# A new written-out order for the first twelve steps, with six weight signs on VectorE, two buffers of C, one of v, and weights laid out by pieces

## The chip, the cores and the metric

The kernel runs on one NeuronCore of one Trainium2 chip. The metric is the device time of one execution in microseconds (us). The kernel before takes 920.79 us, the median of three runs (920.3 to 921.5). The engines are named as in the profile: PE is TensorE, DVE is VectorE, ACT is ScalarE, POOL is GpSimd, SP is the engine that issues the DMAs here.

## The reference, cut to what matters

```python
# attention within chunks of 64 rows: q, k, v are 8 batches x 8 heads x 576 x 64, fp32
scores = q_c @ k_c^T / sqrt(64);  attn = softmax(scores) (sum + 1e-9);  out = attn @ v_c
# heads side by side: x is 4608 x 512; w_in is 512 x 2048, w_out 2048 x 512, both float64
h = x @ w_in
P = a[0] + a[1]*h + a[2]*h**2 + a[3]*h**3
Q = 1 + |b[0]|*|h| + |b[1]|*h**2
y = (P / (Q + 1e-6)) @ w_out          # fp32 out, 4608 x 512
```

## The kernel before, in words

The 4608 rows are cut into 18 blocks of 256 rows, and the 2048 hidden columns into 4 quarters. A block with a quarter is a *step*; there are 72. Each block first needs its attention, each step a first product (ff1), an elementwise chain and a second product (ff2).

Precision comes from splitting: x, the weights and g are each held as a high and a low part in the reduced fp32 type, and a product is three matmuls (high by high, high by low, low by high). One ff1 is 48 matmuls of 128x256 (line 334); one ff2 is counted as 48 rows by the profile (line 405).

The weights arrive as float64 and are turned into the two parts on the chip. They come in 16 pieces of 1 MB: pieces 0-3, 6, 7, 10, 11 are of w_in, the others of w_out, two pieces for each quarter. A piece goes through a buffer called `raw`, of which there are three, shared with the q and k loads of later blocks. On a piece run, in this order: `s` scales the upper words as fp32 (ACT, line 159), `o` shifts the lower words (DVE, line 155), `i` writes the sign of the scaled value over the top of the lower word by a cast to fp16 (ACT, line 163), `j` joins the words to an fp32 value (DVE, line 167), `h` writes the high part (ACT, line 170), and `d` the low part (DVE, line 175). For three pieces the low part is made by PE and ACT instead (`r`, lines 183 and 184, and `l`, line 190). `d` or `r` sets the buffer free, and the next `w` (line 144) that waits for it in SP's queue may then start.

The order of the whole work is fixed. For the first twelve steps (blocks 0 and 1 interleaved, then block 2) and the attention of blocks 0 to 3 it is written out by hand in `START`: every item is a letter and a number, and each engine works through its own items in the order of the list. The other letters: `q`, `v`, `k` load q with k, v, and the constants; `S M U E n N T K A X Y` are the attention of a block (scores, maximum, subtraction, exponential, sums, normalisation, transpose, copy, product with v, high and low part of x); `F f` are the two halves of a step's ff1; `a b c I J` are its ACT part, `Q p P g H R G` its DVE part; `Z z y` are the three parts of its ff2 (the last with the low part of g); `O` stores a block. After the list a loop runs steps 12 to 71 in a fixed pattern, with ff2 two steps behind ff1.

What ties the engines together around the change: the results of ff1 lie in PSUM, bank pair `p0` for steps 0 to 9 save step 1, so that the next ff1 there waits until `P` of the step before has read it; `G`, the last item of a chain on DVE, must come before `y`; tile C of the chain has one buffer, so `c` (line 346) waits until the `R` of the chain before has read it.

Of the kernel before, what the change touches and what calls it, by code (L numbers as in the profile page):

```python
# [9 lines left out]
F32 = mybir.dt.float32  # L10
# [3 lines left out]
ALU = mybir.AluOpType  # L14
# [3 lines left out]
P = 128  # L18
UPB = 2
NB = 18  # L20
BT = 128 * UPB
# [4 lines left out]
FPS = 4  # L26
NST = DFF // (128 * FPS)
W = FPS * BT
# [2 lines left out]
EXP_WIDE = (0, 1)  # L31

START = (
# [12 lines left out]
)  # L46
FIRST = 12
CUT_FIRST, CUT_LAST = 24, 48
# [6 lines left out]
def tile_chunked_attention_rational_moe(  # L55
# [11 lines left out]
    nc = tc.nc  # L67
    cp = ctx.enter_context(tc.tile_pool(name="cp", bufs=1))
    p2 = ctx.enter_context(tc.tile_pool(name="p2", bufs=2))
# [14 lines left out]
    a0, a1, a2, a3 = (ab[:, i:i + 1] for i in range(4))  # L84
    b0, b1a = ab[:, 4:5], ab[:, 6:7]
# [24 lines left out]
    def load_v(n):  # L110
        if n >= NB:
            return
        v = p2.tile([P, W], F32, tag="vt", name=f"v{n}")
        nc.sync.dma_start(out=v, in_=vP[n])
        loaded["v", n] = v

# [18 lines left out]
    def w_load(j):  # L135
        raws[j] = raw = p2.tile([P, W, 2], I32, tag="raw", name=f"raw{j}", bufs=3)
        out, fq, k = PIECES[j]
        if out:
            c = 4 * fq + 2 * k
            src = w_out[c * P:(c + 2) * P, :]  # L140
        else:
            src = w_in[:, 1024 * fq + 512 * k:1024 * fq + 512 * k + 512]
        src = src.rearrange("(c p) (f w) -> p c f w", p=P, w=2)
        nc.sync.dma_start(out=raw.rearrange("p (c f) w -> p c f w", c=src.shape[1]), in_=src)

    def words(j):
        low, high = raws[j][:, :, 0], raws[j][:, :, 1]
        return low, high, high.bitcast(F32)
# [12 lines left out]
    def w_sign(j):  # L161
        upper = raws[j].bitcast(mybir.dt.float16).rearrange("p f (w h) -> p f w h", h=2)[:, :, 0, 1]
        nc.scalar.copy(upper, words(j)[2])  # L163

    def w_join(j):
        low, high, val = words(j)
        nc.vector.scalar_tensor_tensor(high, high, 3, low, ALU.logical_shift_left, ALU.bitwise_or)
# [152 lines left out]
    ch, gbuf, obuf = {}, {}, {}  # L320
# [21 lines left out]
        nc.scalar.activation(ch[n, s][2], ch[n, s][0], AF.Square)  # L342

    def chain_c(n, s):
        ch[n, s][3] = p2.tile([P, FPS, BT], F32, tag="C", name=f"C{n}_{s}", bufs=1)
        nc.scalar.activation(ch[n, s][3], ch[n, s][0], AF.Identity, bias=a2, scale=a3)  # L346

    def chain_q(n, s):
# [96 lines left out]
    def qk(n, u=None):  # L445
# [5 lines left out]
    of_step = lambda f: lambda g: f(*steps[g])  # L451
    do = {
        "k": consts, "B": abs_b1, "q": qk, "v": load_v, "w": w_load,
        "o": w_low, "s": w_scale, "j": w_join, "i": w_sign, "h": w_hi, "d": w_lo_dve, "r": w_rest, "l": w_lo,
        "S": att_s, "M": att_max, "U": att_sub, "E": att_exp, "n": att_rs, "N": att_norm,
        "T": att_t, "K": att_copy, "A": att_av, "X": att_xhi, "Y": att_xlo,
        "O": store,
# [5 lines left out]
    for letter, f in zip("abcQIJpPgHRG", (  # L463
        chain_a, chain_b, chain_c, chain_q, chain_ln, chain_exp,
        chain_p, chain_p2, chain_ghi, chain_r1, chain_r2, chain_glo,
    )):
        do[letter] = of_step(f)
# [9 lines left out]
    for g in range(FIRST, total + LAG):  # L477
        n, s = steps[min(g, total - 1)]
        m, stage = n + 1, s if n + 1 < NB and g < total else None
        one = lambda letters, k: run(" ".join(f"{x}{k}" for x in letters))  # L480
        if g < total:
            one("Ffab", g)
            if stage == 1:
                one("nN", m)
            one("cQ", g)
            if stage == 0:
                one("SMU", m)
                load_qk(m + 1)
            if stage == 2:
                one("A", m)  # L490
                load_v(m + 1)
            one("IJpP", g)
            if stage == 0:
                one("E", m)
            if stage == 2:
                one("X", m)
            one("gHRG", g)
            if stage == 2:
                one("Y", m)
        back = steps[g - LAG]  # L500
        one("Zzy", g - LAG)
        if back[1] == NST - 1:
            store(back[0], last=(back[0] == NB - 1))
        if stage == 1:
            one("TK", m)
# [32 lines left out]
```

## Time and profile before

| | |
|---|---|
| median of the runs | 920.79 us |
| the profiled execution | 920.15 us, of which the span from first to last instruction is 918.3 us |
| PE, DVE, ACT busy in the span | 874.2, 747.0, 593.4 us |
| mean granted TensorE clock | 0.983 of full speed |
| DMA | 55.87 MB in the span |

The span holds one execution; some 1.85 us of the profiled time lie outside of it. Busy times are sums of single instructions with their overlaps taken once. In the rows of groups a number of us is the group's busy time and the number in ns the mean of one instruction. The chain of waits is followed back from the last instruction, and names for each moment what the end was waiting for.

### The profile page before, as it was taken

To read this page: it belongs to the slowest core of one execution; us is meant where nothing else is said; L and a number is where in the kernel's file an instruction comes from. 1 tells how busy PE (TensorE), PEld (TensorE's weight loads), DVE (VectorE), ACT (ScalarE), POOL (GpSimd) and SP (SyncE) were. 2 spreads that over 40 slices of the span, in tenths; PEclk is the share of its full clock that TensorE was granted. 3 is DMA by queue.
4 is the path that set the end of the run, shared out by engine and by line. 5 is a ranking of instruction groups with operands and counts; after the bars stand their busy time and mean duration, and the time that the engine had idled before them with its cause. 6 is when DMAs were issued, how large, how long until landed. Compare 5 with 4: busy or idle time off the path is not lost.

```text
span 918.3 us, 21052 instructions
## 1 busy us (share of the span) xinstructions
PE 874.2 (95%) x9378; PEld 859.6 (94%) x9378; DVE 747.0 (81%) x668; ACT 593.4 (65%) x984; POOL 0.8 (0%) x8
## 2 busy tenths in 40 slices
PE   4579799999999999999999999999999999999997
PEld 2578789999999999999999999999999999999997
DVE  5688888799888878787878787878788887888884
ACT  5999697757575757575757565656565656566452
POOL 0000000000000000000000000000000000000000
PEclk9679999999999999999999999999999999999999
DMA  8443522112010111102020203020202020101011
GB/s 294 164 161 138 170 92 84 27 45 58 36 59 36 41 54 26 69 14 80 4 91 1 93 1 93 2 93 1 93 2 93 2 93 2 47 1 25 1 24 24
DMA packets 20601, 55.87 MB, mean 61 GB/s; under 512 B 2592, under 2 KB 2592, under 8 KB 20512
## 3 DMA queue, kind: packets, MB, share of 16 engines
q1 hardware_dynamic: 20512, 54.54, 18.3%
q8 instruction: 73, 1.20, 0.5%
q14 instruction: 16, 0.13, 0.0%
HBM read 45.09 MB, written 9.44 MB: 59 GB/s over the span
## 4 chain that ended last, share of the span: by engine, by line
PE 82%; ACT 11%; DVE 2%; DMA 2%; issue 1%; SPq 1%; ACTq 0%
PE po L405 39%; PE ph L334 38%; ACT raw L163 3%; PE psx L207 2%; PE pss L207 2%; DMA raw<-in_w_in 2%; ACT raw L159 2%; PE pst L286 1%; ACT e L262 1%; ACT A L339 1%; ACT wo_hi L170 1%; ACT A L354 1%; ACT B L342 1%; ACT C L346 1%; ACT A L358 1%
## 5 line engine op out<-in xcount | busy, mean ns | idle before, releaser
L334 PE MATMUL ph<-xhi,wi_hi 128*128 128x256 f32 x1152 | 325.2, 282 | 10.1 <-DVE C L366 6.7
L334 PE MATMUL ph<-xlo,wi_hi 128*128 128x256 f32 x1152 | 322.3, 280 | 1.6 <-DVE xlo L317 1.6
L334 PE MATMUL ph<-xhi,wi_lo 128*128 128x256 f32 x1152 | 321.5, 279 | 0.0
L339 ACT ACTIVATE A<-ph,ab 128x1024 f32<-128x1024 f32 x72 | 81.1, 1126 | 264.6 <-PE ph L334 263.2
L405 PE MATMUL po<-wo_hi,ghi 128*128 128x256 f32 (+2 forms) x1152 | 228.9, 280 | 3.2 <-DVE ghi L371 3.2
L334 PEld LDWEIGHTS ph<-xhi,wi_hi 128*128 128x128 f32 x1152 | 219.4, 190 | 11.6 <-issue 5.8
L405 PE MATMUL po<-wo_lo,ghi 128*128 128x256 f32 x1152 | 225.6, 277 | 0.0
L334 PEld LDWEIGHTS ph<-xlo,wi_hi 128*128 128x128 f32 x1152 | 219.7, 191 | 2.2 <-DVE xlo L317 2.2
L334 PEld LDWEIGHTS ph<-xhi,wi_lo 128*128 128x128 f32 x1152 | 219.6, 191 | 0.0
L405 PEld LDWEIGHTS po<-wo_hi,ghi 128*128 128x128 f32 x1152 | 174.1, 188 | 5.7 <-DVE ghi L371 3.4
L350 DVE SCALAR_TENSOR_TENSOR B<-B,ab,A 128x1024 f32<-128x1024 f32 x72 | 92.4, 1284 | 103.0 <-ACT B L342 103.0
L405 PEld LDWEIGHTS po<-wo_lo,ghi 128*128 128x128 f32 x1152 | 174.4, 189 | 0.0
L405 PE MATMUL po<-wo_hi,glo 128*128 128x256 f32 (+2 forms) x1152 | 143.3, 277 | 1.6 <-DVE glo L383 1.6
L405 PEld LDWEIGHTS po<-wo_hi,glo 128*128 128x128 f32 x1152 | 136.5, 188 | 2.1 <-DVE glo L383 1.8
L371 DVE SCALAR_TENSOR_TENSOR ghi<-C,ab,A 128x1024 fp32r<-128x1024 f32 x72 | 92.4, 1284 | 11.0 <-ACT A L358 2.4
L354 ACT ACTIVATE A<-B,cst 128x1024 f32<-128x1024 f32 x72 | 83.8, 1165 | 26.3 <-DVE B L350 26.3
L366 DVE SCALAR_TENSOR_TENSOR C<-C,ab,ph 128x1024 f32<-128x1024 f32 x72 | 92.2, 1280 | 3.2 <-ACT B L342 1.0
L379 DVE SCALAR_TENSOR_TENSOR B<-C,ab,B 128x1024 f32<-128x1024 f32 x72 | 92.5, 1284 | 2.4
L383 DVE TENSOR_TENSOR glo<-B,A 128x1024 fp32r<-128x1024 f32 x72 | 88.2, 1225 | 6.8
L362 DVE TENSOR_TENSOR C<-C,ph 128x1024 f32<-128x1024 f32 x72 | 87.5, 1215 | 4.5 <-ACT B L342 3.6
L375 DVE SCALAR_TENSOR_TENSOR B<-B,ghi 128x1024 f32<-128x1024 f32 x72 | 88.2, 1224 | 2.3
L346 ACT ACTIVATE C<-ph,ab 128x1024 f32<-128x1024 f32 x72 | 87.8, 1220 | 2.2 <-DVE B L379 2.0
(53 smaller groups left out, 708.8 us busy)
## 6 DMA issues: line engine op xcount, KB each, us to landing
v<-in_vP SPq DMA_DIRECT2D x18, 512.0 KB, 4.0
out<-o SPq DMA_DIRECT2D x72, 128.0 KB, 2.4
raw<-in_w_in SPq DMA_DIRECT2D x8, 1024.0 KB, 6.6
raw<-in_w_out SPq DMA_DIRECT2D x8, 1024.0 KB, 5.5
qk<-in_qT SPq DMA_DIRECT2D x16, 512.0 KB, 4.6
qk<-in_kT SPq DMA_DIRECT2D x16, 512.0 KB, 5.5
Aqk<-in_qT SPq DMA_DIRECT2D x2, 256.0 KB, 3.6
Bqk<-in_kT SPq DMA_DIRECT2D x2, 256.0 KB, 4.4
```

The costliest lines, as they stand in the source:

```text
L334: nc.tensor.matmul(ph[:, fi, :], w[:, cc, f], x[:, cc, :], start=(k == 0), stop=(k == len(mm) - 1))
L339: nc.scalar.activation(ch[n, s][1], ch[n, s][0], AF.Abs, scale=b0)
L346: nc.scalar.activation(ch[n, s][3], ch[n, s][0], AF.Identity, bias=a2, scale=a3)
L350: nc.vector.scalar_tensor_tensor(B, B, b1a, A, ALU.mult, ALU.add)
L354: nc.scalar.activation(A, B, AF.Ln, bias=cst[:, 0:1], scale=2.0 ** -KLN)
L362: nc.vector.tensor_mul(C, C, h)
L366: nc.vector.scalar_tensor_tensor(C, C, a1, h, ALU.add, ALU.mult)
L371: nc.vector.scalar_tensor_tensor(gbuf[n, s][0], C, a0, A, ALU.add, ALU.mult)
L375: nc.vector.scalar_tensor_tensor(B, B, CQ, gbuf[n, s][0].bitcast(F32), ALU.add, ALU.mult)
L379: nc.vector.scalar_tensor_tensor(B, C, a0, B, ALU.add, ALU.subtract)
L383: nc.vector.tensor_mul(gbuf[n, s][1], B, A)
L405: nc.tensor.matmul(obuf[n][:, i, cols], g[:, fi, i * 128:(i + 1) * 128], w[:, FPS * s + fi, cols], start=start, stop=stop,)
```

## The change: what it does

- The list `START` has the same 383 items save for these: the sign of pieces 2, 3, 4, 5, 10 and 13 is made by a new item `e` on DVE (the sign bit of the upper word is or-ed into the lower word) instead of `i` on ACT; the low part by PE and ACT is made for pieces 6, 7 and 10 instead of 1, 7 and 9, so that `d` moves from 6 and 10 to 1 and 9. All items stand in a new order. It begins with the load of piece 3, and the loads of block 1's q and k and of the constants come later. Pieces are loaded in the order 3, 0, 1, 4, 2, 12, 5, 6, 7, 8, 9, 10, 13, 11, 14, 15; before it was 1, 3, 0, 4, 5, 8, 2, 7, 6, 9, 12, 13, 10, 14, 11, 15.
- Tile C gets two buffers, v one instead of two.
- The host lays out each weight piece as 128 rows of 8 KB. Before, a piece of w_in was read in runs of 2 KB, and one of w_out in runs of 4 KB.

```diff
-    "q0.1 q0.0 w1 q1 S0.0 S0.1 M0.0 U0.0 w3 k0 s1 o1 M0.1 E0.0 U0.1 i1 n0.0 w0 S1 E0.1 j1 n0.1 h1 N0.0 v0 s3 r1 "
-    "o3 M1 v1 i3 N0.1 s0 U1 w4 l1 o0 T0.0 j3 i0 T0.1 K0.0 j0 h3 K0.1 d3 h0 A0.0 w5 E1 d0 A0.1 X0.0 o4 s4 Y0.0 w8 "
-    "n1 X0.1 i4 Y0.1 j4 F0 s5 o5 h4 N1 i5 d4 s8 o8 w2 j5 i8 T1 f0 h5 j8 K1 d5 h8 w7 A1 B0 a0 d8 X1 o2 b0 w6 Y1 s2 "
-    "Q0 F1 c0 v2 o7 i2 p0 s7 j2 I0 o6 f1 P0 i7 J0 j7 h2 g0 a1 d2 Z0 s6 H0 w9 b1 F2 R0 i6 Q1 c1 f2 j6 h7 p1 I1 h6 "
-    "o9 r7 P1 s9 d6 J1 z0 G0 w12 i9 g1 a2 y0 l7 j9 w13 b2 Z1 H1 h9 Q2 z1 s12 R1 I2 o12 r9 c2 G1 J2 p2 y1 i12 w10 "
-    "o13 P2 s13 j12 l9 F4 i13 g2 h12 j13 f4 s10 H2 h13 o10 R2 i10 Z2 a4 d13 c4 z2 G2 b4 p4 y2 Q4 P4 I4 d12 F3 J4 "
...
+    "w3 q0.0 w0 s3 o3 e3 S0.0 q0.1 j3 w1 M0.0 h3 o0 s0 U0.0 d3 S0.1 E0.0 i0 n0.0 w4 M0.1 N0.0 U0.1 s1 j0 T0.0 q1 "
+    "E0.1 o1 h0 n0.1 i1 d0 v0 N0.1 w2 o4 T0.1 K0.0 j1 s4 h1 e4 K0.1 d1 A0.0 j4 w12 A0.1 X0.0 o2 s2 Y0.0 X0.1 e2 "
+    "h4 Y0.1 j2 S1 d4 h2 F0 o12 s12 w5 M1 i12 d2 v1 U1 f0 j12 E1 k0 h12 n1 w6 s5 o5 N1 c0 d12 B0 a0 T1 p0 b0 w7 "
+    "K1 Q0 s6 A1 o6 P0 I0 i6 e5 F2 j5 o7 J0 j6 s7 f2 g0 h6 H0 X1 h5 Z0 Y1 a2 R0 F1 c2 d5 b2 G0 w8 i7 f1 Q2 p2 I2 "
+    "j7 z0 a1 P2 J2 y0 o8 b1 g2 s8 r6 Q1 c1 H2 I1 F3 p1 w9 l6 R2 J1 P1 h7 f3 G2 i8 g1 r7 o9 c3 j8 a3 H1 Z1 w10 h8 "
+    "p3 b3 z1 d8 l7 P3 s9 w13 Z2 Q3 i9 F4 o10 R1 s10 j9 I3 f4 G1 h9 e10 J3 d9 y1 a4 o13 w11 s13 j10 z2 c4 e13 h10 "
...
-        v = p2.tile([P, W], F32, tag="vt", name=f"v{n}")
+        v = p2.tile([P, W], F32, tag="vt", name=f"v{n}", bufs=1)
...
-        src = src.rearrange("(c p) (f w) -> p c f w", p=P, w=2)
-        nc.sync.dma_start(out=raw.rearrange("p (c f) w -> p c f w", c=src.shape[1]), in_=src)
+        nc.sync.dma_start(out=raw.rearrange("p f w -> p (f w)"), in_=(w_out if out else w_in)[2 * fq + k])
...
+    def w_sign_dve(j):
+        low, high, _ = words(j)
+        nc.vector.scalar_tensor_tensor(low, high, -(2 ** 31), low, ALU.bitwise_and, ALU.bitwise_or)
...
-        ch[n, s][3] = p2.tile([P, FPS, BT], F32, tag="C", name=f"C{n}_{s}", bufs=1)
+        ch[n, s][3] = p2.tile([P, FPS, BT], F32, tag="C", name=f"C{n}_{s}", bufs=2)
...
-        "w_in": np.ascontiguousarray(inputs["moe_w_in"]).view(np.int64),
-        "w_out": np.ascontiguousarray(inputs["moe_w_out"]).view(np.int64),
+        "w_in": pieces(inputs["moe_w_in"], (4, P, 8, 256), (2, 1, 0, 3)),
+        "w_out": pieces(inputs["moe_w_out"], (8, 2, P, 512), (0, 2, 1, 3)),
```

More of the change, by code (lines that the diff above doesn't have):

```diff
@@ L137, in w_load @@
         out, fq, k = PIECES[j]
[L138 to L142, printed above, removed]
-        src = src.rearrange("(c p) (f w) -> p c f w", p=P, w=2)
-        nc.sync.dma_start(out=raw.rearrange("p (c f) w -> p c f w", c=src.shape[1]), in_=src)
+        nc.sync.dma_start(out=raw.rearrange("p f w -> p (f w)"), in_=(w_out if out else w_in)[2 * fq + k])
     def words(j):
@@ L453, in tile_chunked_attention_rational_moe @@
         "k": consts, "B": abs_b1, "q": qk, "v": load_v, "w": w_load,
-        "o": w_low, "s": w_scale, "j": w_join, "i": w_sign, "h": w_hi, "d": w_lo_dve, "r": w_rest, "l": w_lo,
+        "o": w_low, "s": w_scale, "j": w_join, "i": w_sign, "e": w_sign_dve, "h": w_hi, "d": w_lo_dve, "r": w_rest, "l": w_lo,
         "S": att_s, "M": att_max, "U": att_sub, "E": att_exp, "n": att_rs, "N": att_norm,
@@ L516, in heads, with pieces @@
         return np.ascontiguousarray(y.transpose(order)).reshape(NB, P, W)
+    def pieces(w, shape, order):
+        w = np.ascontiguousarray(w).view(np.int64).reshape(shape)
+        return np.ascontiguousarray(w.transpose(order)).reshape(8, P, W)
     nc = bacc.Bacc("TRN2", target_bir_lowering=False, num_devices=1, dynamic_dma_scratch_size=1024)
```

12 rows, old and new, of the table START are left out of this document.

## The prediction

> **What bounds the kernel now.** I read the page's 40 slices first, then the busy times by stage, then the chain of waits around the place where PE stops waiting, then the groups of the first stage. The slices:
>
> ```profile
> PE   4579799999999999999999999999999999999997
> ...
> ACT  5999697757575757575757565656565656566452
> ...
> PEclk9679999999999999999999999999999999999999
> ```
>
> PE is full from the eighth slice on; before it has gaps and, in places, a lower clock. The stages, with the limits set where the chain of waits changes (columns: stretch, length, busy us of PE, PEld, DVE, ACT, POOL, granted clock, DMA share, GB/s):
>
> ```profile
> 10.00:100.50 90.50, 63.68 (x563) 56.51 (x563) 73.09 (x78) 85.75 (x71) 0.00 (x0) 0.85 0.49 174
> 100.50:169.80 69.30, 65.75 (x760) 64.15 (x760) 61.44 (x58) 54.69 (x103) 0.00 (x0) 0.98 0.30 100
> 169.80:197.20 27.40, 27.39 (x234) 27.40 (x235) 22.87 (x19) 17.90 (x18) 0.00 (x0) 1.00 0.19 59
> 197.20:907.40 710.20, 710.20 (x7717) 704.76 (x7716) 587.97 (x512) 433.20 (x793) 0.00 (x0) 1.00 0.13 40
> ```
>
> From 10 to 100.5 us ACT is busy 85.75 of 90.5 us: it is the bound. From 100.5 to 169.8 no engine is full. From 169.8 on PE has no gap, and from 197.2 to 907.4 it is busy 710.20 of 710.20 us. The chain says the same (start, us, what the end waited for):
>
> ```profile
> 100.48 7.44 PE ph L334 x48
> ...
> 169.81 5.92 PE ph L334 x48
> ...
> 197.22 5.66 PE ph L334 x48
> 202.88 1.09 PE pss L207 x64
> ...
> 209.82 5.49 PE ph L334 x48
> 215.31 5.45 PE po L405 x48
> 220.75 0.87 PE pst L286 x8
> ...
> 227.09 1.09 PE psx L207 x64
> ```
>
> By the order of the list, 100.48 is F3, 169.81 is F9, and 197.22 is F12, the first matmul of the loop. So the time is 197.2 us of START, then a rest that is PE work without a gap. **Only the end of START on PE can move the time**, for PE's instructions are the same in number before and after.
>
> PE's work in START: 12 ff1 at 5.49, 10 ff2 at 5.45, four blocks' attention at 1.09 + 0.87 + 1.09 = 3.05, three `r` at 2.26 (below): 65.9 + 54.5 + 12.2 + 6.8 = 139.4 us. It ends at 197.2, so 57.8 us are lost. Ahead of F3 stand 8 halves of ff1 (22.0), three ff2 (16.35), two attentions (6.1) and three `r` (6.8): 51.2 us, so 49.3 are lost by 100.5, and 8.5 after it.
>
> ```profile
> 78.67 1.06 PE L183 MATMUL pl<-raw,ident 128*128 128x512 f32 x2
> ...
> 80.93 0.52 PE L405 MATMUL po<-wo_hi,glo 128*128 128x256 f32 x3
> ```
>
> (One `r` is 78.67 to 80.93: 2.26 us.)
>
> **The change part by part.** I compare both lists at a point of equal PE work. In the old list that is F3, which starts when P4 ends. In the new list it is the end of y1: 10 halves of ff1 (27.4), seven parts of ff2 at 1.82 (12.7), two attentions, two `r` (4.5): 50.7 us, 0.5 less. y1 needs G1, the item of DVE just ahead. Now I count what ACT and DVE have to do up to P4 and up to G1. Attention and chain items are the same but for one `I` more; the conversions differ:
>
> - ACT before: 13 `s`, 13 `i`, 12 `h`, 3 `l`. After: 12 `s`, 7 `i`, 10 `h`, 2 `l`.
> - DVE before: 13 `o`, 12 `j`, 8 `d`. After: 12 `o`, 11 `j`, 8 `d`, 4 `e`.
>
> Their prices:
>
> ```profile
> L163 ACT CAST raw<-raw 128x1024 f16<-128x1024 f32 x16 | 42.3, 2646 | 0.2
> L159 ACT ACTIVATE raw<-raw 128x1024 f32<-128x1024 f32 x16 | 20.4, 1272 | 8.7 <-DMA raw<-in_w_in 8.7
> ```
>
> ```profile
> 30.01 1.14 ACT L159 ACTIVATE raw<-raw 128x1024 f32<-128x1024 f32 x1
> 31.05 0.57 ACT L313 CAST xhi<-psx 128x512 fp32r<-128x512 f32 x1
> 31.51 2.57 ACT L163 CAST raw<-raw 128x1024 f16<-128x1024 f32 x1
> 33.73 1.31 ACT L159 ACTIVATE raw<-raw 128x1024 f32<-128x1024 f32 x1
> ```
>
> ```profile
> L167 DVE SCALAR_TENSOR_TENSOR raw<-raw 128x1024 int32<-128x1024 int32 x16 | 19.6, 1227 | 14.3 <-ACT raw L163 14.1
> L155 DVE TENSOR_SCALAR raw<-raw 128x1024 int32<-128x1024 int32 x16 | 11.1, 692 | 1.0 <-DMA raw<-in_w_in 1.0
> ```
>
> On ACT an instruction starts before the one ahead ends: the cast of 2.57 us holds ACT for 33.73 - 31.51 = 2.2 us, the `s` of 1.14 us for 31.05 - 30.01 = 1.04; I take 1.05 for the other passes too. ACT is relieved of 6 x 2.2 + 1.05 + 2 x 1.05 + 1.05 - 1.05 = 16.4 us. Of these, 4 casts are replaced by `e`, two casts and the rest are only put off.
>
> `e` is not in the trace. Its nearest row is `j`, the same operation on the same strided words, 1.23 us, which I take; the ends are `o` with 0.69 and the cast that it replaces with 2.65. DVE gets 4 x 1.23 - 0.69 - 1.23 = +3.0 us (0.8 to 8.7).
>
> **Where the stages begin.** The first weight piece lands late now:
>
> ```profile
> 2.58 0.43 SPq L144 DMA_DIRECT2D raw<-in_w_in  x1
> ```
>
> ```profile
> 10.26 1.17 ACT L159 ACTIVATE raw<-raw 128x1024 f32<-128x1024 f32 x1 [8.25 <-DMA raw<-in_w_in]
> ```
>
> ```profile
> raw<-in_w_in SPq DMA_DIRECT2D x8, 1024.0 KB, 6.6
> raw<-in_w_out SPq DMA_DIRECT2D x8, 1024.0 KB, 5.5
> ```
>
> Issued at 2.58 behind q0, it is there at 10.26. In the new list a weight is the first issue of SP, at 0.73; with 5.5 to 6.6 us to landing it is there at 6.2 to 7.3. I take 7.0 (10.26 if the place in the queue does nothing). q0 now lands behind it, as does w0: both are needed only after piece 3 has gone through `s`, `e` and `j` (1.3 + 1.2 + 1.2 us). The layout may shorten a landing further, as runs of 4 KB land in 5.5 and of 2 KB in 6.6; nothing is in the sum for it, since ACT waited for a piece in only 8.7 us, nearly all of it this first one. In the Trainium skill, the page "DMA: Bandwidth & Descriptors" (sections "Specifications" and "Bandwidth") gives line rate from 512 B on and 6.15 us for 1 MB; by it the new layout is worth nothing, and piece 3 would be there at an estimated 6.9. The trace does not settle this: its two rows differ by 1.1 us, but with other loads in flight.
>
> **The sum.** DVE's work up to P4 is 73.09 less 0.25 for the instruction behind it, and some 0.7 ahead of 10 us: 73.5. Up to G1 it is 76.5. ACT's is 85.75 - 16.4 = 69.4. From 7.0, ACT could be there at 76.4 and DVE at 83.5, so **the bound passes from ACT to DVE**. To DVE's 83.5 come its stalls. ACT as bound stalled 90.5 - 85.75 = 4.75 us in this stage; I take 5 for DVE (0 to 13): G1 at 88.5, y1 with its 1.8 us at 90.3. Against 100.5, less the 0.5 of PE work, that is **9.7 us gained** up to there.
>
> From there PE has 88.7 us to do, and before it took 8.5 longer. At best it goes as from 169.8 to 197.2, which took 27.4 for 26.4 of work, or 3.4 us over 88. The two engines have some more to do after the point than before (two `e` and the conversions put off), C with two buffers lets `c` run before the `R` of the chain ahead, and DVE comes to it with little in hand. I take 6 lost, between 3.4 and 8.5: **2.5 us gained**.
>
> Costed at nothing: C's second buffer and v's loss of one in the loop, under PE's 710.20 of 710.20 us. The load of v now waits in SP's queue until the `A` of the block before has read it; behind it stand loads of q and k and the stores of a block. A block takes four steps of 5.49 + 5.45 us and a load of 1 MB 6.6 to landing, so nearly 40 us of cover would have to go before it cost anything. In START each `v` stands in the list behind the `A` that it waits for. The extra waits of SP for `raw` (the fourth load waits for d3, the sixth for d1) lie in the stalls that I took.
>
> Sum: 920.15 - 9.7 - 2.5 = 907.95 for the profiled execution; the median of the runs is 0.64 above it: **908.6 us**. With `e` at 2.65 us in place of 1.23 DVE would carry 6 x 1.4 = 8.5 us more (917); with piece 3 no earlier than before it would be 3.3 later (911.9).
>
> **The rivals.**
>
> 1. *PE is continuous early.* No stall on DVE up to G1 (y1 at 85.3, 14.7 gained), 3.4 lost after: 5.1 more. 920.8 - 19.8 = 901.0. For it: four of the six `e` stand in the list with other DVE work between their `s` and them. Against it: DVE waited 14.1 us for casts, and ten casts stay.
> 2. *DVE is the bound and stalls as before.* 13 us of stalls up to G1, for it idled 17 of the 90.5: 1.7 gained, and 2.5 after. 920.8 - 4.2 = 916.6. For it: DVE passes from 73.5 to 76.5 us and is already the next fullest.
> 3. *The sign holds up DVE (slower).* A cast followed `s` on the same engine; `e` waits on DVE for an `s` of ACT, and what stands behind it, `P` among them, frees `p0` for the next ff1. If each `e` finds ACT a cast and an `s` behind (2.2 + 1.05), the six cost 6 x 3.25 = 19.5 more: 908.6 + 19.5 = 928. It decides from 2 us of waiting at each `e` (6 x 2 = 12 eats the gain). Against it: ACT has 7 us in hand over DVE at the common point, so that `s` should be early.
> 4. *The change does not do what it says for the time:* the early gain is lost again between F3 and F9, where no engine is full and PE waits for `P`:
>
> ```profile
> PE ph L334 <- DVE C L366: 6.7, 6, 3.6
> ```
>
>    Six such waits, 6.7 us; twice as many and the halved clock after each would take the gain: about 920.
>
> The clock belongs here. F3 took 7.44 us after the longest of these waits, 3.6 us, where ff1 takes 5.49; and between 25 and 30 us, where PE did little, the granted clock is one half:
>
> ```profile
> 25.00:30.00 5.00, 1.98 (x64) 1.79 (x64) 3.96 (x4) 4.89 (x7) 0.00 (x0) 0.50 0.18 17
> ```
>
> So a wait costs up to 2 us more by the clock; this is in the 13 us of rival 2 and in rival 4. The Trainium skill ("TensorE: Matmul & The Clock Gate", Part 1) says that an idle window of about 3.4 us halves the clock; by it waits much below that would cost nothing beyond themselves, and rival 4 would need long ones. The trace agrees so far: 3.6 us came before the slow F3.
>
> **How the numbers follow.** Forecast 0.52, rival 1 0.19, rival 2 0.16, rival 3 0.06, rival 4 0.07. The range reaches from rival 1 past rival 2: 900.5 to 917.5. No change is within 0.2% (1.8 us), about what a measurement of this kernel can tell. Faster holds the forecast and rivals 1 and 2: 0.87; rival 4 makes 0.07 of no change, rival 3 0.06 of slower.
>
> **What would show it.** The first `s` at about 7 us; the cast ten times, and six int32 operations of 1.2 us more on DVE; DVE, not ACT, fullest from 10 to 90 us; the loop's first ff1 at 185 us in place of 197.2; the 710 us of the loop unchanged. It is wrong if `e` takes over 2 us, if DVE's waits for ACT grow past 20 us before the loop, or if PE shows gaps after the loop begins.

## The result and the profile after

The kernel after takes 905.86 us (median of four runs, 904.06 to 906.32) against 920.74 us before (920.3 to 921.5) on the same chip: 14.9 us less, a ratio of 0.9836 with a 95% interval of 0.9824 to 0.9848. Its profiled execution took 906.32 us, with a span of 904.5.

The page's busy tenths in 40 slices, kernel after:

```profile
PE   1589999999999999999999999999999999999997
DVE  6899997898888878887878887878787878878884
ACT  6699996665656666574757475757565656566452
PEclk9989999999999999999999999999999999999999
```

PE is now busy for 90% or more from the fourth slice on; in the row before it was from the sixth. The busy times by stretch of the kernel after (columns as in the prediction: start and end, length, PE, PEld, DVE, ACT, POOL, granted clock, DMA share, GB/s):

```profile
0.00:10.00 10.00, 1.13 (x32) 0.97 (x32) 3.90 (x6) 2.96 (x3) 0.78 (x8) 1.00 0.79 299
30.00:50.00 20.00, 11.82 (x184) 11.11 (x178) 15.75 (x18) 14.55 (x14) 0.00 (x0) 0.87 0.54 185
10.00:90.00 80.00, 57.33 (x599) 53.27 (x600) 73.65 (x79) 69.02 (x62) 0.00 (x0) 0.96 0.48 174
50.10:183.50 133.40, 132.25 (x1299) 127.70 (x1300) 123.62 (x115) 112.03 (x154) 0.00 (x0) 0.99 0.31 108
90.00:100.00 10.00, 10.00 (x74) 8.71 (x73) 10.00 (x11) 9.45 (x10) 0.00 (x0) 1.00 0.50 182
183.50:893.60 710.10, 710.10 (x7719) 704.67 (x7718) 588.43 (x512) 433.49 (x793) 0.00 (x0) 1.00 0.13 40
```

From 10 to 90 us DVE is the fullest (73.65 us, ACT 69.02). But from 50.1 us, where F2 starts, PE has hardly a gap: 132.25 of 133.4 us. The loop takes 710.10 us, all of it PE, as before (710.20). Its first ff1 stands in the chain of waits (start, us, what the end waited for):

```profile
138.64 1.20 DVE C L364
139.85 0.14 issue
139.98 5.90 PE ph L332 x48
...
174.12 9.44 PE po L403 x80
183.56 5.48 PE ph L332 x48
189.04 1.09 PE pss L205 x64
```

183.56 is F12, which before began at 197.22: 13.7 us, and the spans differ by 13.8. So all of the gain was made ahead of the loop. From 139.98 us on the chain runs over PE; between F2 and there it runs over DVE and ACT, although PE idles only 1.15 us in that time. The groups of the conversions up to 180 us (count, busy us, mean ns of one, idle time before them and what ended it):

```profile
L165 DVE SCALAR_TENSOR_TENSOR raw<-raw 128x1024 int32<-128x1024 int32 x16 | 19.5, 1221 | 0.4 <-ACT raw L157 0.3
L161 DVE SCALAR_TENSOR_TENSOR raw<-raw 128x1024 int32<-128x1024 int32 x6 | 7.3, 1223 | 2.0 <-ACT raw L153 2.0
L157 ACT CAST raw<-raw 128x1024 f16<-128x1024 f32 x10 | 25.9, 2588 | 0.1
```

There are ten casts and six `e` (line 161) of 1.223 us, as the change says. The joins (line 165) wait 0.3 us for casts where they waited 14.1.

### The profile page after: what moved, and what is told of

Read it like the earlier page. It is cut to its first block, busy times and chain, and to the rows that moved or that the text cites. A ratio compares the mean times of both kernels' runs of the same rounds, so it can differ in the third digit from the quotient of the medians.

```text
span 904.5 us, 21051 instructions
## 1 busy us (share of the span) xinstructions
PE 865.9 (96%) x9378; PEld 853.7 (94%) x9378; DVE 750.8 (83%) x674; ACT 579.6 (64%) x978; POOL 0.8 (0%) x8
## 4 chain that ended last, share of the span: by engine, by line
PE 84%; DVE 10%; ACT 3%; issue 1%; DMA 1%; DVEq 0%
PE po L403 40%; PE ph L332 39%; PE psx L205 2%; PE pss L205 2%; PE pst L284 2%; DVE raw L165 1%; DMA raw<-in_w_in 1%; DVE C L360 1%; DVE C L364 1%; DVE wo_lo L173 1%; DVE raw L161 1%; DVE B L373 1%; ACT raw L153 1%; DVE ghi L369 1%; DVE B L348 1%
## 5 line engine op out<-in xcount | busy, mean ns | idle before, releaser
L332 PEld LDWEIGHTS ph<-xhi,wi_lo 128*128 128x128 f32 x1152 | 217.2, 189 | 0.0
```

The source lines that it names most:

```text
L332: nc.tensor.matmul(ph[:, fi, :], w[:, cc, f], x[:, cc, :], start=(k == 0), stop=(k == len(mm) - 1))
```

## The experiments

All times are medians; the kernel before took 920.0 to 920.6 us in the comparisons below. Three questions stand in order: which part of the change brought the gain, what bounds the stretch after it, and what is left to be had.

**The order alone.** Each of the six `e` is put back to `i` on ACT, at the same place of the new list.

```diff
-    "w3 q0.0 w0 s3 o3 e3 S0.0 q0.1 j3 ...
+    "w3 q0.0 w0 s3 o3 i3 S0.0 q0.1 j3 ...
```

> The new kernel with all sixteen signs on ACT again (each `e` of the list is an `i` at the same place), all else new. Theory (the bound passed from ACT to DVE, and the order and the signs share the gain): up to y1 ACT gets 4 x 2.2 = 8.8 us more and DVE 4.9 less, so both stand within 5 us of each other and each waits for the other; 907 to 912 us, and the ff1 of step 12 at 185 to 190 us in place of 183.6. Rival A (the order alone makes the gain): 905 to 907. Rival B (the signs alone make it): 915 or more.

Measured: 916.77 us (916.56 to 917.74), ratio 0.9962 (0.9949 to 0.9975); F12 at 194.98 us. Two stretches and a wait (what waited, total us, times, longest) of this kernel:

```profile
90.00:100.00 10.00, 10.00 (x87) 10.00 (x87) 7.08 (x7) 10.00 (x8) 0.00 (x0) 1.00 0.42 160
100.00:110.00 10.00, 6.77 (x25) 4.68 (x24) 6.69 (x7) 9.97 (x10) 0.00 (x0) 0.69 0.18 52
```

```profile
DVE raw L165 <- ACT raw L157: 13.1, 7, 4.8
```

The order by itself gives 3.5 us. Time and F12 lie above the theory's ranges, and the time lies in that of rival B, which the next run does not bear out. ACT is full from 90 to 110 us, the joins wait 13.1 us for its casts, PE runs dry after 100 us and its granted clock falls to 0.69 there.

**The signs alone.** The kernel before, with `i` of pieces 2, 3, 4, 5, 10 and 13 as `e` at the same places of the old list.

```diff
+    def w_sign_dve(j):
+        low, high, _ = words(j)
+        nc.vector.scalar_tensor_tensor(low, high, -(2 ** 31), low, ALU.bitwise_and, ALU.bitwise_or)
...
-    ... o3 M1 v1 i3 N0.1 s0 ...
+    ... o3 M1 v1 e3 N0.1 s0 ...
```

> The kernel before with only six signs moved to DVE: i2, i3, i4, i5, i10 and i13 of the old list become `e` in place; old layout, old buffers. Theory: ACT is the bound up to F3 at 100.5 us and loses 6 x 2.2 = 13 us, DVE gets 6 x 1.2 = 7 us and is then as full as ACT, so half of it is gained: 912 to 917 us. Rival A (the order alone): 919 to 922. Rival B (the signs alone): below 909.

Measured: 914.83 us (914.28 to 916.04), ratio 0.9942 (0.9927 to 0.9957); F12 at 191.74. Its first `s` and a later stretch:

```profile
10.79 1.16 ACT L159 ACTIVATE raw<-raw 128x1024 f32<-128x1024 f32 x1 [8.77 <-DMA raw<-in_w_in]
```

```profile
90.00:100.00 10.00, 6.37 (x53) 6.00 (x52) 10.00 (x9) 5.23 (x5) 0.00 (x0) 1.00 0.37 119
```

The signs alone give 5.5 us. Now DVE is the full engine at 90 to 100 us and PE waits there, after a start that is as late as before. The two edits alone add up to 9.0 us, together they give 14.9 (the layout and the buffers go with the order here): **5.9 us come only from the pair**. The traces suggest why: with the order alone ACT is full from 90 to 110 us, with the signs alone DVE is from 90 to 100, so each seems to leave a bound that the other relieves. The 3.5 us hold for this list, in which six casts stand at the places of `e`; a list arranged for casts was not run.

**The layout alone**, in the old order with the old signs, and **the old layout in the new kernel**.

```diff
-        src = src.rearrange("(c p) (f w) -> p c f w", p=P, w=2)
-        nc.sync.dma_start(out=raw.rearrange("p (c f) w -> p c f w", c=src.shape[1]), in_=src)
+        nc.sync.dma_start(out=raw.rearrange("p f w -> p (f w)"), in_=(w_out if out else w_in)[2 * fq + k])
```

> The kernel before with only the weight pieces laid out as 128 rows of 8 KB; old order, old buffers, signs on ACT. Theory (loads are hidden behind ACT after the first piece; the first piece stands behind q0): first `s` 0 to 1 us sooner than 10.26, time 919.5 to 921.3. Rival (long rows make all loads faster, and that was part of the gain): 915 to 918.5.

> The new kernel with the weights read from memory as before (runs of 2 KB for w_in and 4 KB for w_out), all else new. Theory (only the first piece stands on the path, and it lands little later): first `s` at 6 to 7 us in place of 5.8, 905.5 to 907.5 us. Rival (the new order loads each piece just in time, so the layout is needed): 909 or more.

Measured: 920.41 us (917.54 to 921.38), ratio 0.9998 (0.9987 to 1.0008), with the first `s` at 10.35; and 906.12 us (905.6 to 906.71), ratio 0.9851 (0.9828 to 0.9874), with the first `s` at 6.03. The layout is worth nothing that can be measured in either. With the old layout F2 started at 48.63, 1.4 us sooner than in the kernel after, and F12 still came at 183.97: what is won at F2 need not reach the loop.

**The place of the first weight in SP's queue.** The loads of q and k of block 0, `q0.1` and `q0.0`, are issued ahead of `w3`; nothing else moves.

```diff
-    "w3 q0.0 w0 s3 o3 e3 S0.0 q0.1 j3 w1 ...
+    "q0.1 q0.0 w3 w0 s3 o3 e3 S0.0 j3 w1 ...
```

> The new kernel with the loads of block 0's q and k put ahead of the first weight piece, as before the change; all else new. Theory (the first weight piece decides where DVE's row of work begins, and DVE is the bound from there on): first `s` at 8 to 9.5 us in place of 5.8, and 908 to 909.5 us. Rival (the early start is lost again in the stall for the constants at 40 us): 905.5 to 906.8.

Measured: 910.02 us (909.4 to 910.76), ratio 0.9894 (0.9871 to 0.9916): 4.2 us of the gain gone, half a us more than the theory's range allowed. Its first `s`, and that of the kernel after:

```profile
9.03 1.18 ACT L153 ACTIVATE raw<-raw 128x1024 f32<-128x1024 f32 x1 [7.02 <-DMA raw<-in_w_in]
```

```profile
5.77 1.18 ACT L153 ACTIVATE raw<-raw 128x1024 f32<-128x1024 f32 x1 [3.76 <-DMA raw<-in_w_in]
```

The start is 3.26 us later, F12 3.3 us (186.89 against 183.56). Here the late start came through whole.

**The stall before F2.** From 30 to 50 us DVE is busy 15.75 of 20 us, which is 4.25 of the 6.35 us that it idles from 10 to 90. The order of time in the kernel after there (start, us, engine, line, operation, tiles, and in brackets the idle time before and what ended it):

```profile
33.93 0.43 SPq L437 DMA_DIRECT2D ab<-in_a  x1
...
42.29 1.21 ACT L344 ACTIVATE C<-ph,ab 128x1024 f32<-128x1024 f32 x1 [3.04 <-DMA ab<-in_a]
43.49 1.10 ACT L337 ACTIVATE A<-ph,ab 128x1024 f32<-128x1024 f32 x1
44.63 1.22 DVE L360 TENSOR_TENSOR C<-C,ph 128x1024 f32<-128x1024 f32 x1 [3.09 <-ACT A L337]
45.88 1.02 ACT L340 ACTIVATE B<-ph 128x1024 f32<-128x1024 f32 x1 [1.29 <-DVE C L360]
...
50.07 0.58 PE L332 MATMUL ph<-xhi,wi_hi 128*128 128x256 f32 x1 [0.23 <-DVE C L364]
```

`c0` waits 3.0 us for the chain's constants. The new list issues them at 33.93, right behind two weight pieces and `v1`, and a load of 2 KB then takes some 8 us to land; the old list issued them at 5.61. So `k0` goes right behind `w1`:

```diff
-    ... j3 w1 M0.0 ... E1 k0 h12 ...
+    ... j3 w1 k0 M0.0 ... E1 h12 ...
```

> The new kernel with the load of the constants (`k0`) moved in the list to right behind w1, ahead of the loads that wait for a buffer; all else new. In the new kernel's trace c0 waits 3.0 us for the constants at 42.3 us, a0, p0, b0 and P0 come behind it, and F2 starts only after P0 at 50 us. Theory (from there on DVE is the bound without a gap, so what it stalls counts in full): F2 2.5 to 4 us sooner and 902 to 903.5 us. Rival (PE or ACT sets the end by another way and the time is lost again): within 0.8 us of the new kernel's 905.9.

Measured: 904.15 us (903.7 to 904.82), ratio 0.9825 (0.981 to 0.984). Its F2 and its F12:

```profile
46.81 0.58 PE L332 MATMUL ph<-xhi,wi_hi 128*128 128x256 f32 x1 [0.22 <-DVE C L364]
```

```profile
181.22 5.48 PE ph L332 x48
```

F2 comes 3.3 us sooner, F12 2.3 us, the median is 1.7 us less; the time lies between the two ranges, and the runs of the two kernels overlap (903.7 to 904.82 here, 904.06 to 906.32 after), so the starts of F2 and F12 are the firmer evidence. The constants are the cause of the stall at `c0`, but part of what is won ahead of F2 is lost again behind it.

**Is DVE the bound from F2 on?** The new kernel without the six `e`: the signs of these pieces are left out, so that DVE has 7.3 us less to do.

```diff
-    "w3 q0.0 w0 s3 o3 e3 S0.0 ...
+    "w3 q0.0 w0 s3 o3 S0.0 ...
```

> The new kernel without the six `e`: six weight pieces lose their sign, so the numbers differ and only the time is read. Theory (DVE is the bound up to the loop): each `e` is 1.15 us on the path, four of them ahead of y1, so 4 to 7 us sooner: 899 to 902. Rival (DVE has slack, and the sixteen signs on ACT were the trouble alone): 904.5 to 906.

Measured: 905.15 us (903.82 to 907.02), ratio 0.9836 (0.9808 to 0.9863): within 0.7 us of the kernel after, in the range of the rival and not of the theory. F2 starts at 49.56, F12 at 184.25. The same stretch of time in this kernel:

```profile
50.10:183.50 133.40, 132.22 (x1293) 127.82 (x1292) 119.72 (x111) 111.36 (x153) 0.00 (x0) 0.99 0.31 108
```

DVE is 3.9 us less busy in it and PE just as full. From F2 on the amount of DVE's work does not set the end, although the chain of waits runs over DVE and ACT until 139.98: PE's idle time of 1.15 us in the kernel after leaves little for a freer DVE to win.

**Is it PE, then?** The low parts of pieces 6, 7 and 10 are made by `d` on DVE in place of `r` on PE and `l` on ACT. That takes 3 x 2.26 = 6.8 us off PE and puts three more `d`, of about 1.2 us each, on DVE.

```diff
-    ... g2 s8 r6 Q1 c1 ... w9 l6 R2 ...
+    ... g2 s8 d6 Q1 c1 ... w9 R2 ...
```

> The new kernel with the low part of pieces 6, 7 and 10 made by DVE too: each `r` of the list becomes `d` at the same place and each `l` goes, so PE loses 3 x 2.26 = 6.8 us of work, ACT 2.7, and DVE gets 3 x 1.15 = 3.5 us. Theory formed now (from F2 on PE is the bound: leaving out the six `e` gained nothing, and from F2 at 50.1 to the loop at 183.6 it takes 133.5 us for 127.8 us of work): 899 to 902 us, the loop's first ff1 at 177 to 180. Rival (DVE is the bound from F2 on, as the prediction had it): 907 to 910.

Measured: 909.07 us (908.66 to 909.72), ratio 0.9883 (0.9865 to 0.99): 3.2 us *slower* than the kernel after, which refutes the theory and lies in the range of its rival. F12 comes at 186.68. The same stretch of time, two parts of it, and a row of the timeline:

```profile
50.10:183.50 133.40, 125.70 (x1254) 124.17 (x1254) 124.14 (x116) 107.53 (x149) 0.00 (x0) 0.96 0.32 108
70.00:80.00 10.00, 6.22 (x40) 6.03 (x39) 10.00 (x10) 7.86 (x7) 0.00 (x0) 0.76 0.35 129
90.00:100.00 10.00, 6.87 (x56) 6.70 (x55) 10.00 (x11) 7.88 (x8) 0.00 (x0) 0.96 0.42 138
```

```profile
76.42 0.80 PE L403 MATMUL po<-wo_hi,ghi 128*128 128x256 f32 x2 [3.78 <-DVE ghi L369]
```

PE got gaps where DVE is busy 10.00 of 10 us. So "PE alone" is wrong too. The gaps cost twice: the granted clock over the stretch is 0.96 against 0.99 in the kernel after, which is an estimated 4 us (0.03 of 133.4) and about as much as the whole loss. **Both engines are close to full from F2 on**: taking work from DVE gives next to nothing, because PE is full; moving work from PE to DVE costs, because DVE then makes PE wait, and behind the waits of 3.78 and 3.13 us PE ran at half clock. No run took work from PE without giving DVE more, so what PE alone is worth was not shown.

**More from the stretch ahead of F2.** With the constants early, `K1` and `P0` go ahead of `b0`, so that `p0` is read, and F2 released, sooner.

```diff
-    ... p0 b0 w7 K1 Q0 s6 A1 o6 P0 I0 ...
+    ... p0 K1 P0 b0 w7 Q0 s6 A1 o6 I0 ...
```

> The new kernel with three items moved: the constants right behind w1, K1 ahead of b0, and P0 behind K1, ahead of b0 and Q0. With the constants early alone, F2 began at 46.8 us, behind P0 (46.75) and A1 (46.6); K1 would run at 41.6 while ACT waits for p0, and P0 at 42.6, so that F2 begins at about 44.7. Theory (PE goes without a gap from F2 to the loop, so what F2 gains the end gains): 901 to 903 us. Rival (I0 and what hangs on it come later and cost as much): 904 to 906.

Measured: 903.65 us (903.54 to 903.76), ratio 0.9824 (0.9802 to 0.9846), the fastest kernel that does the whole computation; 2.2 us less than the kernel after, with no overlap of their runs, though their intervals against the kernel before overlap. The time lies between the ranges of the theory and the rival. F2 starts at 44.87, 5.2 us sooner than in the kernel after, F12 at 180.79, 2.8 us sooner. Its stretch from F2 to the loop:

```profile
44.80:180.80 136.00, 132.63 (x1300) 127.34 (x1301) 125.86 (x117) 114.28 (x157) 0.00 (x0) 1.00 0.31 108
```

DVE now carries 125.86 us in it, PE idles 3.4 in place of 1.15. The same two edits as above were tried on this kernel, `d` for `r` and, with the six signs left out, no `e`:

> As the run before (low part of pieces 6, 7, 10 on DVE), and with the constants, K1 and P0 moved as in consts_K1_P0_first (F2 at 44.9 us, 903.65 us). Theory (PE is the bound from F2 on): both gains add, 896.5 to 900 us. Rival (with F2 that early DVE is the bound, since the time from F2 to the loop grew there from 133.5 to 135.9): 902.5 to 906.

> consts_K1_P0_first (903.65 us) without the six `e`, so that six weight pieces lose their sign and only the time is read. Theory (PE is the bound from F2 on, DVE before it, where three `e` stand): F2 1 to 3.5 us sooner than 44.9 and 900.5 to 903 us. Rival A (DVE is the bound after F2 too): 897 to 899.5. Rival B (neither): F2 and the time stay, 903 to 904.5.

Measured: 906.84 us (906.33 to 909.23), ratio 0.9863 (0.9844 to 0.9882), 3.2 us slower than its base and above both ranges; and 903.04 us (902.6 to 903.21), ratio 0.9816 (0.9801 to 0.983), 0.6 us faster, just above the theory's range and inside that of rival B, with F2 at 44.08, 0.8 us sooner. The picture is the same as on the kernel after. In the kernel with K1 and P0 first PE waits 1.6 us for `P`, 1.2 for a `g` and 0.4 for a `Y` between F2 and the loop. Without the six `e` 2.2 us of these 3.2 stay, so the sheer amount of DVE's work does not explain most of them; what does is not settled.

**Which of two readers goes first.** In the kernel after, one of the two longest waits of ACT for DVE before the loop is that of `b` for `p` (both read the same tile in PSUM). It stands here with the wait of `p` for ACT:

```profile
ACT B L340 <- DVE C L360: 6.9, 7, 1.3
...
DVE C L360 <- ACT A L337: 4.3, 3, 3.1
```

In the list `p` stands ahead of `b`, and `b` starts only when `p` has ended (in the timeline above, 45.88 after 44.63 and its 1.22 us). With the constants early, `b` is put ahead of `p` in steps 0, 3, 4, 7, 8, 9 and 10.

```diff
-    ... T1 p0 b0 w7 ... p3 b3 z1 ...
+    ... T1 b0 p0 w7 ... b3 p3 z1 ...
```

> new_consts_early (904.15 us) with `b` put right ahead of `p` in steps 0, 3, 4, 7, 8, 9 and 10. In the new kernel's trace ACT's `b` waits 6.9 us in seven places for DVE's `p`, which stands ahead of it in the list and reads the same PSUM tile. Theory (PE and DVE are both full from F2 on and ACT is not, so these waits of ACT cost nothing and a later `p` does): 904.5 to 907 us, those waits gone from ACT and waits of DVE for `b` in their place. Rival (the waits are on the path): 901 to 903.5.

Measured: 908.74 us (908.43 to 909.0), ratio 0.9876 (0.9859 to 0.9894): 4.6 us slower than with `p` first, the way that the theory had it but beyond its range. Its waits:

```profile
ACT A L352 <- DVE B L348: 13.5, 7, 4.9
DVE C L360 <- ACT B L340: 9.7, 8, 1.8
```

The wait does not go away; it changes sides, from ACT, which has time, to DVE, which has hardly any. Whether the program's own semaphores or the chip keep the two readers apart, no run here tells.

Not tried: the buffers, and the choice of pieces for `r`, apart from the order. With one buffer of C, `c1` would wait for `R2`, which stands on DVE behind `p1`, and `p1` needs `c1`; the new order needs the second C, and the room for it comes from `v`.

## Why the prediction was right in sign and near in size

The time, 905.86, lies inside the range and 2.7 us under the 908.6 forecast; of 14.9 us of gain 12.2 were foreseen. By its steps:

- **The first piece: mis-sized.** Predicted at 7.0 us, it was there at 5.77, and with q0 ahead of it 9.03. The direction and the cause (the place in the queue) hold; the term was 1.2 us too late. The load at the head of the queue was there 5.0 us after its issue at 0.73, under the 5.5 to 6.6 that I took from the medians of all pieces, most of them with others in flight.
- **The price of `e`**: 1.23 us taken from `j`, 1.223 measured. DVE's work from the start to G1 was 3.90 + 73.65 - 2.1 (from 87.9 to 90) = 75.4 us against 76.5; 0.2 of it lie ahead of the first piece.
- **The stalls of DVE up to G1: mis-sized, and their cause was not named.** From 5.8 to 87.9 us there are 82.1 us for 75.2 of work: 6.9 stalled, where I took 5. 4.25 of them lie between 30 and 50 us, with the wait for the constants, 3.1, as their largest part; 2.0 are waits of `e`. The diff shows that this load moves; I put it down under "the extra waits of SP lie in the stalls" and did not follow which instruction would need it. With it early the kernel gains 1.7 us.
- **The common point**: G1 predicted at 88.5, measured 87.90; y1 predicted to end at 90.3, measured 90.6. Gained up to there: 100.48 less 0.5, less 90.6, is 9.4 us; 9.7 were predicted. The early start (1.2) and the smaller work (1.3) outweigh the longer stall (1.9), so G1 came 0.6 us early. But the step from G1 to y1 was wrong here: the prediction let y1 start when G1 ends, and it started 0.84 us later, right behind a matmul of an ff1, so PE and not G1 held it. That the end of y1 came within 0.3 us of the forecast is partly luck. The row of G1 in the chain, and y1 in the timeline with what stands around it:

```profile
86.76 1.13 DVE glo L381
```

```profile
88.62 0.28 PE L332 MATMUL ph<-xhi,wi_lo 128*128 128x256 f32 x1
88.74 2.05 PE L403 MATMUL po<-wo_hi,glo 128*128 128x256 f32 x16
90.63 0.42 PE L403 MATMUL po<-wo_hi,ghi 128*128 128x256 f32 x2
```

- **After it**: 183.56 - 90.6 = 93.0 us for 88.7 of PE work, so 4.3 lost, between my ends of 3.4 and 8.5 and under the 6 that I took. F12 came at 183.56 where 185 was forecast. Another 1.1 us of the 2.7 lie in how the runs spread: I set the median 0.64 above the profiled execution, and here it lies 0.46 under it.
- **"The bound passes from ACT to DVE"** is right up to F2 and too simple after it. The prediction took DVE's work up to G1 as one stage; the trace has two. Up to F2 PE waits for the conversions and the first chain. From F2 on PE has eleven ff1, ten ff2, two attentions and three `r` to do, 60.4 + 54.5 + 6.1 + 6.8 = 127.8 us by the prediction's prices. At the rate of 27.4 for 26.4, which it took from a stretch without gaps, that is 132.6 of the 133.4 us it took. That the prediction still came so near to y1 fits two engines that are full at once, as at 90 to 100 us, where both are busy 10.00 of 10: reckoned on either, the end is nearly the same.
- **A misreading that changed nothing:** the prediction called PE full from the eighth slice of the kernel before; the row has 90% or more from the sixth. No term was built on it.
- **The rivals.** Rival 1, PE continuous early (901.0): half of it came. After y1 4.3 us were lost, near its 3.4, but ahead of G1 DVE stalled 6.9 us, where it has none. Rival 2, DVE stalls of 13 us: 6.9. Rival 3, the sign holds up DVE: `e` waited 2.0 us in all, not 19.5 (in the list five of the six, and not four, have other DVE work between their `s` and them). Rival 4, the gain lost at `P`: PE waited 1.4 us in three such places up to the loop, after 6.7 in six:

```profile
PE ph L332 <- DVE C L364: 1.4, 3, 0.8
```

- **The layout at nothing** is borne out twice, 920.41 us against 920.3 before and 906.12 against 905.86 after. In the Trainium skill, the page "DMA: Bandwidth & Descriptors" (section "Specifications") puts line rate at 512 B and more; nothing in these runs, with 2, 4 and 8 KB, speaks against it: with the longer rows the first `s` goes from 10.26 to 10.35 us in the old order and from 6.03 to 5.77 in the new.
- **What I had no term for** is the interplay: the parts of the sum stand beside each other as if each could be had alone. The total came out, but the runs give 3.5 us to the order, 5.5 to the signs, and 5.9 to the two together.

## What to carry to other kernels

Where two engines take turns as the bound, an edit that frees one of them can be worth more when the other is freed too: cost the pair together, and test each alone to see who is full then. In a list written out by hand, follow every load that moves to the first instruction that needs it, the smallest loads too: a few KB behind megabytes cost 3 us of ACT and DVE here. And where two engines read one tile and one waits for the other, look which of the two has time: here the other order only moved the wait to the fuller engine, at 4.6 us.

## What the runs showed of the hardware that was not expected

- **A load of 2 KB is not quick when others are in flight.** The DMA issues of the kernel after, and behind them those of the kernel with the constants right behind `w1` (KB each, us from issue to landing):

```profile
ab<-in_a SPq DMA_DIRECT2D x1, 2.0 KB, 8.3
```

```profile
ab<-in_a SPq DMA_DIRECT2D x1, 2.0 KB, 9.5
```

  That is longer than the 1 MB piece at the head of the queue took, 5.0 us.
- **A gap of 3.13 us was followed by half the clock.** In the kernel with the low parts on DVE, PE idled from 95.9 to 99.03 us; the granted clock is 1.00 to 99 us and then:

```profile
99.03 0.48 PE L332 MATMUL ph<-xhi,wi_hi 128*128 128x256 f32 x1 [3.13 <-DVE C L364]
```

```profile
99.00:100.00 1.00, 0.97 (x5) 1.00 (x6) 1.00 (x2) 0.00 (x0) 0.00 (x0) 0.55 0.80 279
100.00:102.00 2.00, 2.00 (x11) 2.00 (x11) 2.00 (x3) 1.23 (x2) 0.00 (x0) 0.50 0.86 352
```

  The prediction cited the Trainium skill ("TensorE: Matmul & The Clock Gate", Part 1) for an idle window of about 3.4 us; this gap, of 3.13 us between matmuls whose ends are modelled and of 3.30 us between weight loads, lies just under that, and the measurement decides.
